# Loads of keys, values and output weights issued by GpSimd's DMA queue instead of SyncE's, in a one-core decode kernel

## The chip, the core and the metric

The kernel runs on one core of one Trainium2 chip. The metric is the device time of one execution in microseconds (us); the kernel before takes 1325.38 us, the median of three runs that lie between 1325.36 and 1325.40 us.

## The reference

One token for each of two batch elements passes through an attention block with a long cache and through a small MLP block; a gate mixes the two. Cut to what matters:

```python
# x (2,1,1024); k_cache, v_cache (2,32,16384,128); wq (1024,4096); wo (4096,1024)
# w1, w2 (1024,1024); w3 (1024,3584); w4 (3584,1024), all bfloat16
g = sigmoid((x * gate_w).sum(-1, keepdims=True))
q = (x @ wq) as (2 batch, 32 heads, 1, 128)
scores = einsum("bhqd,bhkd->bhqk", q, k_cache) * 128 ** -0.5
o = einsum("bhqk,bhkd->bhqd", softmax(scores), v_cache)
a = (o as (2, 1, 4096)) @ wo
h = gelu(layernorm(x) @ w1)              # its four column blocks are shifted along a
hs = concat(shifted blocks of h) @ w2    # sequence of length 1, so that zeros remain
x1 = x + hs
b = x1 + gelu(layernorm(x1) @ w3) @ w4
out = g * a + (1 - g) * b
```

Keys and values are 268.4 MB each (2 x 32 x 16384 x 128 x 2 bytes); all weights that are loaded together are some 34 MB.

## The kernel before

**Tiling.** The 64 pairs of batch element and head are worked on two heads of one batch element at a time, so there are 32 rounds, `n` = 0 to 31. A round needs one tile of keys and one of values. Each is a single load of 128 rows (partitions) of 64 KB, 8192 KB in all; a head takes 64 partitions, with 256 positions in each.

**The ring.** All large loads land in `ring`, five slots of 32 KB in each partition. A tile of keys or values takes two slots: values always slots 0 and 1, keys slots 3 and 4 in even rounds and 2 and 3 in odd ones (`k_slots`). The two halves of a key tile are used in an order (`k_order`) that frees slot 3 first. The weights take one slot each (`w_slots`): wq in 0 and 1, w2 in 2, w3 in 3 and 4, w4 in 0 and 1 again, and at the end wo in 4 and 3. w1 isn't loaded, since the shift leaves zeros.

**Loads.** `queue_load` puts every load into one list in the order of its use: wq (two loads), w2, w3 (two), w4 (two), then K(0), V(0), K(1), V(1) and so on, and wo (first half one load, second half six pieces). `pump` (L305) takes loads from the head of that list as long as their slots are free, and gives each the events it has to wait for: the last matmul that read the slot. `release`, called where the program writes such a matmul down, frees the slot and calls `pump` again. So a load's instruction stands in its engine's program at the place where its slots are released in the order of writing, and waits there for TensorE. Each slot has a semaphore (`s_ring`), each piece of wo one of `s_tail`.

**Prologue.** TensorE computes q from wq (L622), the zero rows from w2 (L510), the w3 product from both halves of w3 (L478), and the w4 product into rows (L510, 56 matmuls for each half). VectorE then adds and scales these rows (`st_bg`, L526 and L529). The last matmul on the first half of w3 and the one on the second free the slots of K(0); the last one on w4 frees those of V(0).

**A round.** GpSimd writes the query columns into `Z` (L652, two instructions; from the second round on they wait until the scores of the round before are done). VectorE transposes the key tile in place in eight pieces (L665); TensorE forms scores from each piece (L671, 64 matmuls in all; after 32 of them the first of the two slots is released, which is what K(n+1) waits for). Then comes the softmax (L681 to L698), the product with values (`do_PV`, L707, 64 matmuls, whose last one frees the slots for V(n+1)) and a small output step (`do_out`, L716 to L721). TensorE, VectorE and ScalarE run their rounds in a loop of 16 passes of two rounds; SyncE and GpSimd have them written out.

**End.** `do_aproj` multiplies the attention output with wo (L746), VectorE copies the rows (L775) and four small stores write them out.

SyncE issues every large load; ScalarE issues six small ones at the start (x and the gate weights) and two of the four stores; GpSimd issues none. After its constants GpSimd has one instruction in the prologue (L442) and the 64 of `Z`.

## Time and profile before

| what | before |
|---|---|
| median of three runs | 1325.38 us |
| span of the profiled execution, first to last instruction | 1323.6 us |
| time around the span, median less span | 1.8 us |
| moved by DMA | 570.6 MB, 431 GB/s over the span |
| packets of SyncE's DMA queue, share of 16 DMA engines | 99.7% |
| TensorE matmul busy | 784.8 us, 59% |
| VectorE busy | 660.1 us, 50% |
| ScalarE busy | 45.7 us, 3% |
| GpSimd busy | 23.6 us, 2% |
| granted TensorE clock, mean | 0.79 |

The profile covers one execution of the program. Its time is taken as the span and what lies around it: a change of the span is carried over to the median by adding the same 1.8 us. A row of the chain of waits or of the timeline begins with its start and its length in us. "SPq" is SyncE's instruction queue and "ACTq" ScalarE's; their rows are the issue of a load and not its transfer. Busy time of an engine counts neither issues of loads nor waits.

### The profile page before, as it was taken

To read this page: it belongs to the slowest core of one execution; us is meant where nothing else is said; L and a number is where in the kernel's file an instruction comes from. 1 tells how busy PE (TensorE), PEld (TensorE's weight loads), DVE (VectorE), ACT (ScalarE), POOL (GpSimd) and SP (SyncE) were. 2 spreads that over 40 slices of the span, in tenths; PEclk is the share of its full clock that TensorE was granted. 3 is DMA by queue.
4 is the path that set the end of the run, shared out by engine and by line. 5 is a ranking of instruction groups with operands and counts; after the bars stand their busy time and mean duration, and the time that the engine had idled before them with its cause. 6 is when DMAs were issued, how large, how long until landed. Compare 5 with 4: busy or idle time off the path is not lost.

```text
span 1323.6 us, 12296 instructions
## 1 busy us (share of the span) xinstructions
PE 784.8 (59%) x5235; PEld 335.4 (25%) x5235; DVE 660.1 (50%) x527; ACT 45.7 (3%) x99; POOL 23.6 (2%) x110
## 2 busy tenths in 40 slices
PE   3645557655556765555676554566656457656546
PEld 2512223222222322222232222222222222222223
DVE  1154446655444665544466554446655445665443
ACT  0000000000000000000000000000000000000000
POOL 3000000000000000000000000000000000000000
PEclk9966787777678777767877877888786788878679
DMA  9999999999999999999999999999999999999998
GB/s 404 444 422 436 436 430 434 436 434 432 434 438 432 430 442 430 430 440 430 430 440 430 430 440 430 432 438 430 434 436 430 436 436 428 440 432 438 432 430 365
DMA packets 11409, 570.60 MB, mean 431 GB/s; under 512 B 1267, under 2 KB 1795, under 8 KB 1926
## 3 DMA queue, kind: packets, MB, share of 16 engines
q1 hardware_dynamic: 11368, 570.43, 99.7%
q8 instruction: 8, 0.13, 0.0%
q14 instruction: 3, 0.02, 0.0%
q10 hardware_dynamic: 30, 0.01, 0.0%
HBM read 570.44 MB, written 0.00 MB: 431 GB/s over the span
## 4 chain that ended last, share of the span: by engine, by line
DMA 69%; PE 24%; DVE 6%; issue 1%; SPq 0%; POOL 0%
DMA ring<-in_A_k_cache_dram 65%; PE ps L671 23%; DVE ring L665 6%; DMA ring<-in_A_wo_dram 2%; DMA ring<-in_A_wq_dram 2%; PE ps L478 1%; PE ps L622 0%; DVE hsd L548 0%; PE ps L510 0%; PE ps L401 0%; SPq L329 0%; SPq L335 0%; POOL mv L442 0%; DVE orow L775 0%; DVE q_f L634 0%
## 5 line engine op out<-in xcount | busy, mean ns | idle before, releaser
L671 PE MATMUL ps<-ring,Z 128*128 128x512 bf16 x2048 | 533.6, 419 | 389.8 <-DVE ring L665 389.3
L665 DVE STREAM_TRANSPOSE ring<-ring 128x2048 f32<-128x2048 f32 x256 | 565.2, 2275 | 277.8 <-DMA ring<-in_A_k_cache_dram 277.8
L671 PEld LDWEIGHTS ps<-ring,Z 128*128 128x128 bf16 x2048 | 203.4, 104 | 707.5 <-issue 471.6
L707 PE MATMUL ps<-ring,PT_sb 128*32 128x512 bf16 x2048 | 168.2, 501 | 3.9 <-DVE recip L698 3.5
L721 DVE SCALAR_TENSOR_TENSOR OT_sb<-ps,gT,recip 128x2 f32 x32 | 7.0, 219 | 203.2 <-PE ps L718 203.2
L707 PEld LDWEIGHTS ps<-ring,PT_sb 128*32 128x32 bf16 x2048 | 67.6, 122 | 90.5 <-issue 69.1
L692 ACT ACTIVATE P_sb<-ps,negm 128x512 bf16<-128x512 f32 x32 | 22.0, 687 | 1013.9 <-DVE negm L690 1013.9
L681 DVE TENSOR_REDUCE rA<-ps 128x1 f32<-128x512 f32 x32 | 22.1, 692 | 64.1 <-PE ps L671 64.1
L696 PE MATMUL ps<-rowsum,hsel 128*128 128x1 f32 x128 | 24.4, 294 | 38.0 <-ACT P_sb L692 38.0
L694 DVE STREAM_TRANSPOSE PT_sb<-P_sb 128x512 bf16<-128x512 bf16 x32 | 22.8, 712 | 27.0 <-ACT P_sb L692 27.0
L652 POOL TENSOR_TENSOR Z<-q_f,mask 128x8 bf16<-128x8 f32 x64 | 12.3, 228 | 1212.9 <-PE ps L671 1212.9
L696 PEld LDWEIGHTS ps<-rowsum,hsel 128*128 128x128 f32 x128 | 21.7, 240 | 40.7 <-ACT P_sb L692 40.7
L683 PE MATMUL ps<-ident,rmax_bf 128*1 128x128 bf16 x32 | 6.9, 217 | 33.1 <-DVE rmax_bf L682 33.1
L716 ACT ACTIVATE acc_sb<-ps 128x512 bf16<-128x512 f32 x32 | 19.1, 597 | 199.0 <-PE ps L707 199.0
L718 PE MATMUL ps<-dsel,acc_sb 128*128 128x2 bf16 x128 | 8.1, 167 | 22.5 <-ACT acc_sb L716 22.5
L478 PE MATMUL ps<-xn_bf,ring 128*128 128x2 bf16 x224 | 14.5, 202 | 1.4 <-DVE xn_bf L444 1.4
L718 PEld LDWEIGHTS ps<-dsel,acc_sb 128*128 128x128 bf16 x128 | 5.3, 96 | 38.3 <-ACT acc_sb L716 38.3
L683 PEld LDWEIGHTS ps<-ident,rmax_bf 128*1 128x1 bf16 x32 | 2.5, 79 | 48.9 <-DVE rmax_bf L682 48.9
L478 PEld LDWEIGHTS ps<-xn_bf,ring 128*128 128x128 bf16 x224 | 14.4, 172 | 1.5 <-issue 1.4
L622 PE MATMUL ps<-xT_bf,ring 128*128 128x2 bf16 x256 | 7.1, 165 | 12.2 <-DVE xT_f L605 7.9
L684 DVE TENSOR_REDUCE m_sb<-ps 1x2 bf16<-1x128 bf16 x32 | 8.9, 279 | 9.9 <-PE ps L683 9.9
L690 DVE TENSOR_SCALAR negm<-ps,cAB 128x1 f32<-128x1 f32 x32 | 8.9, 278 | 9.2 <-PE ps L687 9.2
(98 smaller groups left out, 88.9 us busy)
## 6 DMA issues: line engine op xcount, KB each, us to landing
ring<-in_B_w_dram SPq DMA_DIRECT2D x4, 3584.0 KB, 35.3
ring<-in_A_wq_dram SPq DMA_DIRECT2D x2, 4096.0 KB, 17.5
ring<-in_A_wo_dram SPq DMA_DIRECT2D x1, 4096.0 KB, 40.2
ring<-in_B_w_dram SPq DMA_DIRECT2D x1, 2048.0 KB, 27.3
ring<-in_A_wo_dram SPq DMA_DIRECT2D x1, 2048.0 KB, 22.3
ring<-in_A_wo_dram SPq DMA_DIRECT2D x1, 1024.0 KB, 24.4
ring<-in_A_k_cache_dram SPq DMA_DIRECT2D x32, 26.9
ring<-in_A_v_cache_dram SPq DMA_DIRECT2D x32, 29.2
```

The source lines that it names most:

```text
L478: fn = lambda e, nb=nb, kl=kl: e.matmul(out_ps[:, nb, :], lhsT=cols(wv, kl, nb, nout), rhs=rhs_of(k0 + kl), start=False, stop=True, skip_g ...
L652: ev = pl.add("pool", lambda e, hp=hp: e.tensor_tensor(Z[:, :, ZO:ZO + P].rearrange("p t (i c) -> p t i c", c=32)[:, :, 2 * hp:2 * hp + 2, ...
L665: return pl.add("dve", lambda e: e.transpose(ap, ap), waits=(arrived(("k", n)),), sig=True)
L671: ev = pl.add("pe", lambda e, bp=bp: e.matmul(S_ps[:, 0:NCOL], lhsT=Z[:, bp, ZO - 2 * u:ZO - 2 * u + P], rhs=kv[:, :, bp // 2, :, bp % 2], ...
L681: e1 = pl.add("dve", lambda e: e.tensor_reduce(rA[:, :], S_ps[:, 0:NCOL], axis=AX.X, op=ALU.max), waits=(ev_S[n],), sig=True)
L683: e3 = pl.add("pe", lambda e: e.transpose(mt_ps, rmax_bf[:, :], ident[:, :]), waits=(e2,), sig=True)
L692: e7 = pl.add("act", lambda e: e.activation(P_sb[:, :], S_ps[:, 0:NCOL], ACT.Exp, bias=negm[:, 0:1], scale=scale, accum_out=rowsum[:, 0:1] ...
L694: e8 = pl.add("dve", lambda e: e.transpose(PT_sb[:, :], P_sb[:, :]), waits=(e7,), sig=True)
L696: e9 = pl.add("pe", lambda e, hp=hp: e.matmul(l_ps[:, hp:hp + 1], lhsT=hsel[:, hp, :], rhs=rowsum[:, 0:1], start=True, stop=True, skip_gro ...
L707: ev = pl.add("pe", lambda e, jj=jj, cg=cg: e.matmul(acc_ps[32 * cg:32 * cg + 32, 0:512], lhsT=PT_sb[:, 32 * jj:32 * jj + 32], rhs=vv[:, 4 ...
L716: e1 = pl.add("act", lambda e: e.activation(acc_sb[:, :], acc_ps[:, 0:512], ACT.Copy), waits=(ev_pv,), sig=True)
L718: e2 = pl.add("pe", lambda e, w=w: e.matmul(oT_ps, lhsT=acc_sb[:, w * P:(w + 1) * P], rhs=dsel[:, w, :], start=(w == 0), stop=(w == 3)), w ...
```

## The change

The loads of keys, values and wo move from SyncE's program to GpSimd's, with semaphores of their own for the slots (`s_pool`). wq, w2, w3 and w4 stay with SyncE, as do the two stores. Order of the list, slots, waits and sizes are the same.

```diff
         s_ring = [sem(f"dr{i}") for i in range(NRS)]
+        s_pool = [sem(f"dp{i}") for i in range(NRS)]
...
                 for k, fn in enumerate(fns):
-                    dsem = s_ring[slots[0]] if len(fns) == 1 else s_tail[k]
-                    dma_done[key] = dma_done[key, k] = pl.dma("sp", (lambda e, fn=fn, idx=slots[0]: fn(e, idx)), dsem,
+                    eng = "pool" if key[0] in ("k", "v", "wo") else "sp"
+                    dsem = (s_pool if eng == "pool" else s_ring)[slots[0]] if len(fns) == 1 else s_tail[k]
+                    dma_done[key] = dma_done[key, k] = pl.dma(eng, (lambda e, fn=fn, idx=slots[0]: fn(e, idx)), dsem,
                                                               waits=waits if k == 0 else ())
```

The line numbers of the changed kernel are higher by two from there on (L361 of before is L363). GpSimd's program from the end of the prologue into the first rounds, before; L442 is the last step of the layer norm, L652 writes `Z`, `e_pe` counts TensorE's steps:

```order
L280 MEMSET xrow 128x256 [waits e_pool]
L442 TENSOR_TENSOR mv<-mv,neg_half 128x2 [waits e_pool,e_dve]
L652 TENSOR_TENSOR Z<-q_f,mask 128x4x2 x2
L652 TENSOR_TENSOR Z<-q_f,mask 128x4x2 [waits e_pe]
L652 TENSOR_TENSOR Z<-q_f,mask 128x4x2
```

The same place in the changed kernel; L363 is a tile of keys and L367 one of values:

```order
L444 TENSOR_TENSOR mv<-mv,neg_half 128x2 [waits e_pool,e_dve]
L363 DMA ring<-in_A_k_cache_dram 128x32768 [waits e_pe]
L367 DMA ring<-in_A_v_cache_dram 128x32768 [waits e_pe]
L654 TENSOR_TENSOR Z<-q_f,mask 128x4x2 x2
L363 DMA ring<-in_A_k_cache_dram 128x32768 [waits e_pe]
L367 DMA ring<-in_A_v_cache_dram 128x32768 [waits e_pe]
L654 TENSOR_TENSOR Z<-q_f,mask 128x4x2 x2
```

K(0) and V(0) now stand ahead of the first `Z`, and K(n+1) and V(n+1) between `Z` of round n and `Z` of round n+1. `Z` of round n+1 has lost its own wait, since V(n+1) ahead of it waits for a later step of TensorE.

SyncE's whole program in the changed kernel; L331 are the weights, L780 the stores:

```order
L796 UNCONDITIONAL_BRANCH [waits barrier_Pool_Activation_PE_DVE_SP_release]
L331 DMA ring<-in_A_wq_dram 128x16384 x2
L331 DMA ring<-in_B_w_dram 128x8192
L331 DMA ring<-in_B_w_dram 128x14336 x2
L331 DMA ring<-in_B_w_dram 128x14336 [waits e_pe] x2
L780 DMA out_dram<-orow 2x256 [waits e_dve] x2
L168 UNCONDITIONAL_BRANCH [waits dout0,dout1]
```

Before, the loads of keys, values and wo stood between the two loads of w4 (the fifth row) and the stores. So w4 and K(0) were on one queue and are now on two. GpSimd's program at its end, in the changed kernel:

```order
L363 DMA ring<-in_A_k_cache_dram 128x32768 [waits e_pe]
L367 DMA ring<-in_A_v_cache_dram 128x32768 [waits e_pe]
L331 DMA ring<-in_A_wo_dram 128x16384
L654 TENSOR_TENSOR Z<-q_f,mask 128x4x2 x2
L331 DMA ring<-in_A_wo_dram 128x8192 [waits e_pe]
L331 DMA ring<-in_A_wo_dram 128x4096
L331 DMA ring<-in_A_wo_dram 128x2048
L337 DMA ring<-in_A_wo_dram 128x2x512
L337 DMA ring<-in_A_wo_dram 128x512 x2
```

The six pieces of the second half of wo stand behind the last `Z`; nothing is behind them.

## The prediction

> **What bounds the kernel now.** I read the page first, for the share of the DMA engines:

> ```profile
> span 1323.6 us, 12296 instructions
> DMA  9999999999999999999999999999999999999998
> q1 hardware_dynamic: 11368, 570.43, 99.7%
> HBM read 570.44 MB, written 0.00 MB: 431 GB/s over the span
> DMA 69%; PE 24%; DVE 6%; issue 1%; SPq 0%; POOL 0%
> ```

> The DMA engines are full in every slice, and nearly all of it is SyncE's queue (q1). The chain of waits gives PE 24%, but that is not work which could be saved, as its pieces in order of time show:

> ```profile
> 53.30 29.12 DMA ring<-in_A_k_cache_dram
> 82.42 0.02 issue
> 82.45 2.32 DVE ring L665
> 84.77 0.13 issue
> 84.90 9.99 PE ps L671 x32
> 94.91 26.22 DMA ring<-in_A_k_cache_dram
> ...
> 559.22 26.32 DMA ring<-in_A_k_cache_dram
> 597.36 26.88 DMA ring<-in_A_k_cache_dram
> 635.49 27.45 DMA ring<-in_A_k_cache_dram
> ...
> 1255.70 26.47 DMA ring<-in_A_k_cache_dram
> ```

> A load of keys lands at start plus length: K(0) at 82.42, the last at 1282.17. That is 1199.75 us for 31 rounds, 38.70 us a round. A round moves two tiles of 8.389 MB, so the stream runs at 433.5 GB/s and one tile takes 19.35 us. A load is under way for 26.2 us or more, so it was issued 7 us or more before its bytes could start: the transfer ahead of it was still running. **Full queue** is what bounds the kernel; the 1323.6 us of the span are 570.4 MB at 433.5 GB/s (1316 us) and some 8 us at both ends.

> What the change can do is therefore: make the stream run dry somewhere (each us of that is a us of time), change its rate, or nothing. How far ahead a load is issued comes from the timeline of two rounds and from the line views of the two loads (keys first, then values):

> ```profile
> 585.56 17.66 DVE L665 STREAM_TRANSPOSE ring<-ring 128x2048 f32<-128x2048 f32 x8 [7.61 <-DMA ring<-in_A_k_cache_dram]
> 597.36 0.33 SPq L361 DMA_DIRECT2D ring<-in_A_k_cache_dram  x1
> 605.28 0.39 POOL L652 TENSOR_TENSOR Z<-q_f,mask 128x8 bf16<-128x8 f32 x2 [38.31 <-PE ps L671]
> 614.38 0.33 SPq L365 DMA_DIRECT2D ring<-in_A_v_cache_dram  x1
> 624.27 17.66 DVE L665 STREAM_TRANSPOSE ring<-ring 128x2048 f32<-128x2048 f32 x8 [8.51 <-DMA ring<-in_A_k_cache_dram]
> 626.71 10.61 PE L671 MATMUL ps<-ring,Z 128*128 128x512 bf16 x40 [11.42 <-DVE ring L665]
> DMA to landing us min/median/max: 26.2/26.9/29.1
> DMA to landing us min/median/max: 27.9/29.2/35.4
> ```

> Less the 19.35 us of its own transfer, a load of keys has a lead of 6.9 to 9.8 us, one of values 8.5 us or more.

> **Part by part: the rounds.** Let L be the time from the end of GpSimd's wait to the first byte of its load. No row of the trace shows a load by GpSimd. From below the nearest row is SyncE's issue, 0.33 us. From above it is the longest way that a small load of another queue has taken, in the timeline of the start:

> ```profile
> 0.74 0.56 ACTq L577 DMA_DIRECT2D xg_row<-in_A_x_dram  x1
> 0.74 0.88 SPq L329 DMA_DIRECT2D ring<-in_A_wq_dram  x2
> 1.33 0.23 ACTq L578 DMA_DIRECT2D xg_row<-in_gate_w_dram  x1
> 7.87 0.62 PE L600 MATMUL ps<-ident,xg_row 3*128 3x3 bf16 x8 [7.87 <-DMA xg_row<-in_gate_w_dram]
> 24.24 3.57 PE L622 MATMUL ps<-xT_bf,ring 128*128 128x2 bf16 x128 [4.32 <-DMA ring<-in_A_wq_dram]
> ```

> The 2 KB of the gate weights took 6.5 us from issue at 1.33 to TensorE's start at 7.87, landing and company of another queue included, which L has not. I take L = 2 us, nearer to the lower end for that reason. [...]

> With L between 0.33 and 6.5 us the rounds lose nothing: the smallest lead is 6.9 us. The 64 issues cost SyncE's time, which nobody waits for, and now GpSimd's, which has 38.31 us of idle time ahead of each `Z`. The new place of `Z` costs nothing either. It stands behind V(n+1), which waits for the product with values: SyncE's issue at 614.38 marks that moment, so `Z` comes at 614.4 + 2 + 0.4 = 616.8 us, and its user, the matmul at 626.71, starts 9.9 us later. If that cover went, each us over it would cost a us a round, 31 in all.

> **The prologue.** Here two loads that were behind one another on one queue are now on two. The first row is from the list of issues (w4 is among these four loads), the others are from the timeline:

> ```profile
> ring<-in_B_w_dram SPq DMA_DIRECT2D x4, 3584.0 KB, 35.3
> 53.30 0.33 SPq L361 DMA_DIRECT2D ring<-in_A_k_cache_dram  x1
> 55.38 3.15 PE L510 MATMUL ps<-ring,GT_bf 128*2 128x256 bf16 x56 [2.11 <-DVE GT_bf L462]
> 63.15 3.15 PE L510 MATMUL ps<-ring,GT_bf 128*2 128x256 bf16 x56 [4.61 <-DMA ring<-in_B_w_dram]
> 66.35 0.33 SPq L365 DMA_DIRECT2D ring<-in_A_v_cache_dram  x1
> 66.36 1.77 DVE L526 TENSOR_TENSOR bgrow<-ps,xrow 2x256 f32<-2x256 f32 x4 [11.12 <-PE ps L510]
> 68.17 1.00 DVE L529 TENSOR_SCALAR ps<-bgrow,grow 64x256 f32<-64x256 f32 x2
> ```

> The second half of w4 landed at 63.15. Its 3.67 MB take 8.47 us at 433.5 GB/s, so it ran from 54.7; K(0), issued at 53.30, had to wait for it and ran from 63.1 to 82.42. Both together keep the engines busy until 82.5 in any order. But V(0) can only be issued when TensorE has used w4, and in the rounds nothing else is ready: K(1) waits for scores of K(0). If K(0), on a queue of its own, no longer stands behind w4, then w4 lands later, V(0) is issued later, and the stream may run dry at 82.5.

> That queues share the engines the start shows: the gate weights were through at 7.87 us, although SyncE's two loads of 4.19 MB, issued before, needed until 24.24. How two large loads share isn't shown; I bound it. From below, w4 goes first, lands at 63.15 as now, and the loss is 0. From above, K(0) goes first altogether and w4 lands at 82.5. The page of the profile counts 11368 packets on q1, which is one packet for each contiguous row of a load and 16 more for each load (10112 rows in 78 loads, and 8 for the stores). So w4 is 8 packets of 1.06 us on each of 16 engines, and K(0) 8 of 2.42 us. I take turns packet by packet. K(0) comes at 53.30 + 2 = 55.3, in the first packet of w4; from there the packets alternate, and the eighth of w4 ends at 54.7 + 8 x 1.06 + 7 x 2.42 = 80.1 us. TensorE's 56 matmuls take 3.15 us, V(0) is free to be issued at 83.3, its first byte comes at 85.3, and the engines have been empty since 82.5: **2.8 us** lost. By the upper bound it is 82.5 + 3.2 + 2 - 82.5 = 5.2 us. With L = 3 us two packets of w4 are through before K(0) comes, and it is 1.4; from L = 4 on it is nothing.

> [...]

> The shift has a second user, which adds nothing: VectorE's 2.8 us of L526 and L529 come at 83.3 instead of 66.36 and hold up the first transpose from 82.45 to 86.1, so scores are 3.6 us later and K(1) is issued at 98.5. V(0) then runs until 104.7, so K(1) is still 6 us early.

> **The end.** The second row is from the chain of waits in order of time, the others are from the timeline:

> ```profile
> 1282.19 17.66 DVE L665 STREAM_TRANSPOSE ring<-ring 128x2048 f32<-128x2048 f32 x8 [10.19 <-DMA ring<-in_A_k_cache_dram]
> 1293.84 0.33 SPq L329
> 1295.15 1.68 SPq L335 DMA_DIRECT2D ring<-in_A_wo_dram  x3
> 1320.62 0.91 PE L746 MATMUL ps<-ring,OT_sb 128*2 128x256 bf16 x8 [0.28 <-DMA ring<-in_A_wo_dram]
> 1321.05 0.95 DVE L775 CAST orow<-ps 34x256 bf16<-34x256 f32 x2 [7.42 <-PE ps L746]
> ```

> Behind the last keys (1282.2) the stream still has V(31), until 1301.5, and the first 4.19 MB of wo, until 1311.2. The pieces of the second half, issued by SyncE until 1296.8, may come 14 us later before the engines wait. Six of them at 2 us each on GpSimd after the wait at 1293.8 are issued by 1305.8: cost 0. Without that cover it would be 12 us.

> **The sum.** 1323.6 + 2.8 = 1326.4 us of span, with 1.8 us around it 1328.2 us, against a median of 1325.38. I call 0.2% (2.65 us) no change, about what a measurement of this kernel can tell; the forecast lies just beyond it.

> **Rivals.** *The stream doesn't run dry:* w4 lands early enough, because queues share by bytes (each gets half the rate, w4 then lands at about 71 and V(0) is issued at 74.5) or because GpSimd's first load takes 4 us. Then nothing changes: 1325.4 us. For it speaks that a queue's first load is the slow one at ScalarE (0.56 us to issue, the second 0.23), and that the early landing of the gate weights shows sharing but not how; against it, that a packet is the only unit of which the trace tells.

> *VectorE holds GpSimd up.* K(n+1) is issued in the middle of the eight transposes (597.36 within 585.56 to 603.22). If GpSimd could not write its load's program until they are done, the round would be 17.66 us of transposes, L, and 19.35 us of transfer: 37.0 + L. That decides from L = 1.7 us on. At L = 2 it is 0.3 us a round, 9 us in all (1335); at L = 3 it is 1.3 us a round, 40 us (1366). No row shows GpSimd at work during a transpose, so the trace says neither yes nor no. [...] A transpose of 2048 elements takes 2.2 us here (17.66 for eight), just under one element a ns.

> *The software queue is slower itself.* If one of 16 engines lags by 0.5 to 2%, each tile does, and 64 tiles of 19.35 us make 6 to 25 us: 1332 to 1350. No row speaks for it. [...]

> *Faster:* the change from one load to the next costs SyncE's queue something, and GpSimd's less. At 0.3% of the 1238 us of tiles that is 3.7 us: 1321.7. No row shows a gap between tiles, so little is to be had.

> **Chances.** The forecast (a gap of 1.4 to 5.2 us, L up to 3 us; 1326.8 to 1330.6) has 0.50; no dry stream 0.22; VectorE's hold 0.10; a slower queue 0.08; a faster one 0.10. Of the forecast's 0.50 I put 0.29 above 1328.03 us, the bound of 0.2%. So slower is 0.29 + 0.10 + 0.08 = 0.47, same 0.21 + 0.22 = 0.43, faster 0.10. The range reaches from 1324, which leaves out the faster case (0.10), to 1340, which takes in the small ends of the two slow cases and leaves out some 0.10.

> **What would show it.** In the changed kernel's timeline the second group of L512 (L510 of before) starts at about 80 and not at 63, V(0) is issued at 83, and a slice near 83 to 85 us has idle DMA engines; from there everything is later by the same amount, with rounds of 38.70 us. L is read off at the first load that finds the engines empty. A round of more than 38.8 us proves the prediction wrong and one of the two slow rivals right: VectorE's hold if keys start only after the last transpose, the queue if tiles take over 19.4 us while two are in flight. L512 at 63 us with the old time means that nothing ran dry.

## The result and the profile after

The changed kernel takes 1328.03 us (median of 18 runs, 1327.42 to 1328.79), the kernel before 1325.40 us (18 runs beside them, 1325.24 to 1325.55). The ratio is 1.002, with a 95% interval from 1.0014 to 1.0026: slower by 2.6 us, just at the bound of 0.2%. The profiled execution has a span of 1326.6 us, 3.0 more than before. The forecast was 1328.2 us and 1326.4 us of span. So the total is as forecast; its parts are not, as the rest shows, and that the total agrees is in part luck.

The page of the changed kernel, its lines on DMA and the shares of the chain:

```profile
span 1326.6 us, 12296 instructions
DMA  9999999999999999999999999999999999999998
q0 software_dynamic: 9968, 545.26, 95.1%
q1 hardware_dynamic: 1016, 25.17, 4.5%
DMA 68%; PE 24%; DVE 6%; issue 1%; POOL 0%; SPq 0%
```

The stream now is GpSimd's queue (q0), and it is as full as SyncE's was (430 GB/s over the span, 431 before). A loss of 3 us does not show in slices of 33 us. It shows in the chain of waits, in order of time, where a load of keys lands at start plus length:

```profile
53.45 29.00 DMA ring<-in_A_k_cache_dram
94.14 28.39 DMA ring<-in_A_k_cache_dram
134.66 26.58 DMA ring<-in_A_k_cache_dram
...
1179.44 26.89 DMA ring<-in_A_k_cache_dram
1217.58 28.11 DMA ring<-in_A_k_cache_dram
1257.73 26.68 DMA ring<-in_A_k_cache_dram
```

| landing | before | after | later by |
|---|---|---|---|
| K(0) | 82.42 | 82.45 | 0.03 |
| K(1) | 121.13 | 122.53 | 1.40 |
| K(2) | 159.82 | 161.24 | 1.42 |
| K(29) | 1204.76 | 1206.33 | 1.57 |
| K(30) | 1243.47 | 1245.69 | 2.22 |
| K(31) | 1282.17 | 1284.41 | 2.24 |
| end of span | 1323.6 | 1326.6 | 3.0 |

The loss thus comes in three steps: 1.40 us between K(0) and K(1), 0.65 in one late round, and 0.8 behind the last load. The 28 rounds from K(1) to K(29) add 0.17 us together. The first step is in the timeline of the changed kernel:

```profile
53.45 0.73 POOL L363 DMA_DIRECT2D ring<-in_A_k_cache_dram  x1 [15.20 <-PE ps L480]
75.23 3.15 PE L512 MATMUL ps<-ring,GT_bf 128*2 128x256 bf16 x56 [16.98 <-DMA ring<-in_B_w_dram]
78.72 0.54 POOL L367 DMA_DIRECT2D ring<-in_A_v_cache_dram  x1 [24.54 <-PE ps L512]
82.47 17.66 DVE L667 STREAM_TRANSPOSE ring<-ring 128x2048 f32<-128x2048 f32 x8 [1.22 <-DMA ring<-in_A_k_cache_dram]
```

The second half of w4 is there at 75.23 us (63.15 before), V(0) is issued at 78.72 (66.35 before), and the transposes start as soon as K(0) lands. The rows of the view of DMA that count the packets started from 78 to 98 us, first before, then after:

```profile
DMA packets 145, 8.45 MB, mean 423 GB/s; under 512 B 16, under 2 KB 16, under 8 KB 16
```

```profile
DMA packets 133, 7.62 MB, mean 381 GB/s; under 512 B 16, under 2 KB 16, under 8 KB 16
```

Thirteen packets of 64 KB are missing in this stretch, and there is one fetch of instructions more, of 16 KB at 80.1 us (five of the thirteen come in the next 20 us, where the starts fall otherwise): here the stream loses its time. In the records of single packets the engines end K(0) one by one between 79.9 and 82.1 us, and V(0)'s first packets start between 80.2 and 82.2, so that between the two loads an engine goes 0.35 us on average without a packet of either. But nearly all of the first two packets of V(0) on each engine take 2.5 to 3.9 us instead of 2.42, and that is another 1.15 us an engine. Most of the loss is slow first packets, and only the smaller part is engines that stand empty. K(0) is used 0.4 us after the last engine is through with it (82.07 and 82.47 us), so a landing can be later by more or less than the 16 engines are on average; here K(1) is 1.40 us later by its landing and 1.37 by the average.

The last step is at L168, where each engine has a DRAIN and behind it an EVENT_SEMAPHORE. Before, then after:

```profile
L168 POOLq DRAIN  x1: 486/486/486, 1263.2 to 1263.2; - x1
L168 SPq DRAIN  x1: 7/7/7, 1323.4 to 1323.4; - x1
```

```profile
L168 POOLq DRAIN  x1: 28295/28295/28295, 1298.1 to 1298.1; - x1
L168 SPq DRAIN  x1: 7/7/7, 1325.7 to 1325.7; - x1
```

GpSimd's DRAIN took half a microsecond in the middle of the last rounds; now it takes 28.3 us and ends at 1326.4, after SyncE's, so that all wait for it: the EVENT_SEMAPHOREs of the other four, at 1323.6 before, are at 1326.5 and 1326.6. Its end lies 3.41 us behind the last packet of the software queue (1322.97). K(31) is 2.24 us late and SyncE's DRAIN 2.3, so nearly all of the 0.8 us behind the last load is this wait.

### The profile page after: what moved, and what is told of

Its sections match the earlier page's. It is cut to its first block, busy times and chain, and to the rows that moved or that the text cites. A ratio compares the mean times of both kernels' runs of the same rounds, so it can differ in the third digit from the quotient of the medians.

```text
span 1326.6 us, 12296 instructions
## 1 busy us (share of the span) xinstructions
PE 784.0 (59%) x5235; PEld 333.9 (25%) x5235; DVE 659.9 (50%) x527; ACT 45.7 (3%) x99; POOL 62.9 (5%) x181
## 2 busy tenths in 40 slices
DMA  9999999999999999999999999999999999999998
## 3 DMA queue, kind: packets, MB, share of 16 engines
HBM read 570.44 MB, written 0.00 MB: 430 GB/s over the span
## 4 chain that ended last, share of the span: by engine, by line
DMA 68%; PE 24%; DVE 6%; issue 1%; POOL 0%; SPq 0%
DMA ring<-in_A_k_cache_dram 65%; PE ps L673 22%; DVE ring L667 6%; DMA ring<-in_A_wo_dram 2%; DMA ring<-in_A_wq_dram 2%; PE ps L480 1%; PE ps L624 0%; DVE hsd L550 0%; PE ps L512 0%; PE ps L403 0%; POOL ring L331 0%; PE ps L748 0%; POOL mv L444 0%; DVE orow L777 0%; DVE q_f L636 0%
## 5 line engine op out<-in xcount | busy, mean ns | idle before, releaser
L363 POOL DMA_DIRECT2D ring<-in_A_k_cache_dram x32 | 18.3, 573 | 649.2 <-PE ps L673 634.0
L367 POOL DMA_DIRECT2D ring<-in_A_v_cache_dram x32 | 16.9, 528 | 540.1 <-PE ps L709 515.6
L512 PE MATMUL ps<-ring,GT_bf 128*2 128x256 bf16 x112 | 6.1, 406 | 19.2 <-DMA ring<-in_B_w_dram 17.0
L624 PE MATMUL ps<-xT_bf,ring 128*128 128x2 bf16 x256 | 7.1, 165 | 12.1 <-DVE xT_f L607 7.9
## 6 DMA issues: line engine op xcount, KB each, us to landing
ring<-in_B_w_dram SPq DMA_DIRECT2D x4, 3584.0 KB, 38.9
```

Of the source, the lines that this page charges most:

```text
L363: queue_load(("k", n), [lambda e, idx: e.dma_start(ring[:, idx:idx + 2, :].rearrange("p s m -> p (s m)"), kv_src(A_k, n))], k_slots[n % 2])
L367: queue_load(("v", n), [lambda e, idx: e.dma_start(ring[:, idx:idx + 2, :].rearrange("p s m -> p (s m)"), kv_src(A_v, n))], (0, 1))
```

## The experiments

Three questions were open: whether two queues or the software queue cost the 1.4 us; how long before the engines run out a load has to be issued; and what ties the DRAIN down.

### One queue or two

**K(0) on ScalarE's queue**, no load on GpSimd:

```diff
-                    dma_done[key] = dma_done[key, k] = pl.dma("sp", (lambda e, fn=fn, idx=slots[0]: fn(e, idx)), dsem,
+                    dma_done[key] = dma_done[key, k] = pl.dma("act" if key == ("k", 0) else "sp", (lambda e, fn=fn, idx=slots[0]: fn(e, idx)), dsem,
```

> The kernel before, with K(0) alone issued on ScalarE's hardware queue; GpSimd issues nothing. Theory now (what costs is that K(0) and w4 are on two queues, whichever they are: w4 lands late, V(0) is issued within 2 us of the first engine's running empty, and its first packets are slow): w4 lands at 75 to 80 us, V(0) is issued at 78 to 83, K(1) lands 1.4 us late or more, 1326.8 to 1328.5, as with K(0) alone on GpSimd (1327.0). Rival (it is the software queue): 1325.4.

```profile
77.51 3.01 PE L510 MATMUL ps<-ring,GT_bf 128*2 128x256 bf16 x56 [19.01 <-DMA ring<-in_B_w_dram]
80.57 0.33 SPq L365 DMA_DIRECT2D ring<-in_A_v_cache_dram  x1
122.94 8.89 DVE L665 STREAM_TRANSPOSE ring<-ring 128x2048 f32<-128x2048 f32 x4 [9.30 <-DMA ring<-in_A_k_cache_dram]
```

Measured: 1327.68 us (11 runs, 1327.19 to 1328.11), ratio 1.0017 (1.0008 to 1.0026). In its timeline w4 is late, and K(1) is used at 122.94, 1.8 us later than before. So this much is lost with SyncE's and ScalarE's queues too, without a load on GpSimd's.

**K(0) alone on GpSimd**, all else on SyncE (GpSimd passes its arrival on to the semaphore that the others wait for):

```diff
+                    eng = "pool" if key == ("k", 0) else "sp"
...
+                pl.add("pool", lambda e: e.sem_inc(s_ring[k_slots[0][0]], 16), waits=tuple(fwd))
```

> Only K(0) is issued by GpSimd; V(0), all later tiles and wo stay with SyncE. Theory (the stream loses time because V(0) is issued late, with w4 held up by K(0), and then needs GpSimd's long way to its first byte): w4 still lands at about 75 us, but SyncE issues V(0) at 78.5 and needs 1.0 us to the first byte (as its first load of the kernel: issue 0.74, first packet 1.77), so V(0) is there before the first engine is empty at 79.9. K(1) lands at 121.1 to 121.4 as before, and the time is 1325.4 to 1325.8. Rival 1 (two queues that share cost time by themselves, whoever issues V(0)): K(1) at 122.5, 1326.8. Rival 2 (GpSimd's queue costs in the rounds and at the end): 1325.4.

```profile
75.06 3.16 PE L517 MATMUL ps<-ring,GT_bf 128*2 128x256 bf16 x56 [16.52 <-DMA ring<-in_B_w_dram]
78.26 0.33 SPq L372 DMA_DIRECT2D ring<-in_A_v_cache_dram  x1
84.84 17.66 DVE L672 STREAM_TRANSPOSE ring<-ring 128x2048 f32<-128x2048 f32 x8 [3.76 <-POOLq L767]
97.18 0.33 SPq L368 DMA_DIRECT2D ring<-in_A_k_cache_dram  x1
```

Measured: 1327.03 us (1325.66 to 1327.70), ratio 1.001 (1.0001 to 1.0019). The theory, that nothing is lost when SyncE issues V(0), fell: SyncE issues it at 78.26, 0.04 us behind the last matmul on w4 (GpSimd takes 0.34), and in the profiled run (1327.10 us) K(1) is as late as in the changed kernel (1.45 us). The first rival stood, but not for all of the loss: averaged over the 16 engines K(1) is only 0.73 us late (1.37 in the changed kernel), and five of the eleven runs took 1326.15 us or less, the other six 1327.03 or more. So with SyncE as the issuer about half of the average loss is left; the other half went with the issuer or with the 0.5 us by which V(0) is issued earlier, which no run tells apart. The end costs nothing here: K(31) is 1.65 us late and the span 1.7 us longer, and GpSimd's DRAIN takes 0.58 us. The transposes start late because the last of K(0)'s 4-byte packets (more on these below) came at 84.47, behind a packet of V(0); K(1) is issued at 97.18 for that reason, and its packets lose nothing by it.

**w4 on GpSimd too**, one queue for w4 and K(0), but w3 on the other:

```diff
-                    eng = "pool" if key[0] in ("k", "v", "wo") else "sp"
+                    eng = "pool" if key[0] in ("k", "v", "wo", "w4") else "sp"
```

> As the changed kernel, but w4 too is loaded by GpSimd, so that w4 and K(0) are on one queue again, one behind the other, and w4 shares the engines with wq, w2 and w3 on SyncE's queue. Theory (two queues alternate packet by packet, and a load that frees the next one is slowed): w3, which frees K(0)'s slots, now lands at about 62 us instead of 46, K(0) is issued at about 70, the stream has run dry since 63, and K(0) lands at 92 to 94 instead of 82.4; everything is later by about 11 us, and the time is 1335 to 1338 us. Rival 1 (the loss of the changed kernel is that w4 and K(0) were on different queues, and nothing else): then it is gone, 1325.4 to 1326.2 us. Rival 2 (a queue that was first keeps its turn, so that w3 is hardly slowed): 1326 to 1329 us.

The timeline, and the row of a table by stretches whose last columns are the granted clock, the share of the DMA engines and GB/s:

```profile
63.20 7.26 PE L480 MATMUL ps<-xn_bf,ring 128*128 128x2 bf16 x112 [3.46 <-DMA ring<-in_B_w_dram]
70.76 0.57 POOL L363 DMA_DIRECT2D ring<-in_A_k_cache_dram  x1 [27.17 <-PE ps L480]
94.27 17.66 DVE L667 STREAM_TRANSPOSE ring<-ring 128x2048 f32<-128x2048 f32 x8 [13.19 <-DMA ring<-in_A_k_cache_dram]
```

```profile
66.00:72.00 6.00, 4.46 (x71) 4.37 (x69) 1.05 (x6) 0.25 (x1) 0.57 (x1) 1.00 0.00 0
```

Measured: 1338.31 us (4 runs, 1338.12 to 1338.56), ratio 1.0098 (1.0082 to 1.0113), 0.3 us above the range. The landings are 11.8 us late from K(0) to K(31). Now w3 is the load that is slowed, the load behind it comes 17 us later, and the engines stand still. This is the mechanism of the prologue with a loss eight times as large: a load that frees the slots of the next one is slowed by one that could have stood behind it.

**All but wq on GpSimd**, so that w4 and K(0) are on one queue and w3 as well:

```diff
-                    eng = "pool" if key[0] in ("k", "v", "wo") else "sp"
+                    eng = "sp" if key[0] == "wq" else "pool"
```

> As the changed kernel, but w2, w3 and w4 are loaded by GpSimd too, ahead of K(0) in the same queue; only wq stays with SyncE. Theory (two queues with large loads cost, and the software queue by itself only the end): w2 is issued at about 15.2 us, when GpSimd has written its constants, still during wq; from about 25 us one queue feeds the engines, in the order of before. w4 lands at 63 to 64 us, V(0) is issued at 66 to 67 and K(0) and K(1) land within 0.3 us of before (82.4 and 121.1). Only the 0.8 us of the last DRAIN are left: 1325.9 to 1326.5 us, with runs that lie within 0.4 us. Rival 1 (the software queue as such costs the start, with whatever it stands beside): K(1) is 1.4 us later than before and the time 1327.6 to 1328.6 us, as in the changed kernel.

```profile
63.25 3.16 PE L512 MATMUL ps<-ring,GT_bf 128*2 128x256 bf16 x56 [4.60 <-DMA ring<-in_B_w_dram]
66.73 0.54 POOL L367 DMA_DIRECT2D ring<-in_A_v_cache_dram  x1 [12.47 <-PE ps L512]
121.28 8.89 DVE L667 STREAM_TRANSPOSE ring<-ring 128x2048 f32<-128x2048 f32 x4 [8.50 <-DMA ring<-in_A_k_cache_dram]
```

Measured: 1326.67 us (11 runs, 1326.36 to 1328.38), ratio 1.0011 (1.0002 to 1.002), span 1324.7. The landings are as the theory has them: w4 at 63.25, all keys 0.13 to 0.15 us later than before. The software queue by itself costs 0.14 us at the start, nothing in the rounds, and about 1.0 us at the end. The median is 0.2 us above the expected range and the runs spread over 2 us; the profiled run shows no reason for the spread.

### When the load comes

**K(0) waits until the gelu result is written** (55.3 us), 2.4 us later than in the changed kernel:

```diff
-                       k_slots[n % 2])
+                       k_slots[n % 2] + (("gate",) if n == 0 else ()))
...
-        put([gelu2])
+        def open_gate():
+            slot_free["gate"] = (evd["GT"],)
+            pump()
+        put([gelu2, open_gate])
```

> The changed kernel with K(0) held until the gelu result (55.3 us). Theory: K(0) is issued at 55.5 and its first packet comes 4 us later, when one or two packets of w4 are left on each engine: w4 lands at 66 to 68 us, V(0) is issued at 70 to 71, 9 us before an engine is empty, so neither K(0) nor V(0) comes to an engine that has run out. K(1) lands at 121.1 to 121.5, and only what is lost outside the prologue stays: 1326.0 to 1326.8. Rival (a first load by GpSimd costs its 1.4 us in any place): 1328.0.

```profile
55.86 0.73 POOL L363 DMA_DIRECT2D ring<-in_A_k_cache_dram  x1 [17.62 <-DVE GT_bf L464]
70.28 3.16 PE L512 MATMUL ps<-ring,GT_bf 128*2 128x256 bf16 x56 [11.75 <-DMA ring<-in_B_w_dram]
73.77 0.54 POOL L367 DMA_DIRECT2D ring<-in_A_v_cache_dram  x1 [17.18 <-PE ps L512]
121.06 11.08 DVE L670 STREAM_TRANSPOSE ring<-ring 128x2048 f32<-128x2048 f32 x5 [8.49 <-DMA ring<-in_A_k_cache_dram]
```

Measured: 1326.09 us (11 runs, 1326.03 to 1326.27), ratio 1.0005 (0.9996 to 1.0014), as expected. More packets of w4 go ahead of K(0) than in the changed kernel; w4 lands at 70.28 us, later than the expected 66 to 68, and V(0) is issued at 73.77, still early enough: all landings up to K(31) are those of before within 0.1 us. What is left is the end. This is the fastest kernel with GpSimd's loads, 1.9 us below the changed one and 0.7 above before.

**K(0) waits until the first half of w4 is used** (58.6 us); the gate is the same, opened there:

```diff
+            if key == ("w4", 0):
+                slot_free["gate"] = (ev,)
```

> All of the changed kernel, but K(0) waits in addition until the first half of w4 has been used (58.5 us), so that with 4 us to its first byte it comes as the second half of w4 ends. Theory: no sharing, w4 lands at 63 to 64 us, V(0) is issued at 67, K(1) lands at 121.1 to 121.6, the 1.4 us of the prologue are gone, and 1.2 us of the 2.6 stay: 1326.6. If all that was lost came from the prologue: 1325.4. Rival (it is spread over rounds and end, the prologue being chance): 1328.0.

```profile
58.92 0.73 POOL L365 DMA_DIRECT2D ring<-in_A_k_cache_dram  x1 [20.68 <-PE ps L514]
62.96 3.16 PE L514 MATMUL ps<-ring,GT_bf 128*2 128x256 bf16 x56 [4.36 <-DMA ring<-in_B_w_dram]
84.29 17.66 DVE L669 STREAM_TRANSPOSE ring<-ring 128x2048 f32<-128x2048 f32 x8 [15.31 <-DMA ring<-in_A_k_cache_dram]
```

Measured: 1328.25 us (1327.12 to 1328.93), ratio 1.0021 (1.0012 to 1.003), against 1326.6 expected. w4 and V(0) are in time now, but K(0), issued 4.0 us before w4 was through, lands 1.85 us late: coming so shortly before the other queue is empty loses as much here as the changed kernel does (1.40).

**K(0) waits for w4 to land, on GpSimd's queue and on SyncE's.** The same edit on the changed kernel and on the one before:

```diff
+                if key == ("k", 0):
+                    waits += (dma_done["w4", 1],)
```

> The changed kernel with K(0) held until the second half of w4 has landed (63.15 us): the stream is dry for as long as GpSimd's load needs to start. Theory (time from dry to the first byte is 4.05 us as at K(0), and two first packets are slow by 0.6 us each): K(0) lands 5.3 us later than the 82.4 of before, and this passes whole to the end: 1325.4 + 5.3 + 1.2 = 1331.9. With 1.6 us, the shortest that V(0) shows: 1329.5. Rival (a delay of the stream is made up later): 1326 to 1327.

> The kernel before with K(0) held in the same way, issued by SyncE. Theory (1.0 us to the first byte, one first packet slow by 0.65 us): K(0) lands 1.8 us later, 1327.2. The difference to the kernel with GpSimd is the price of a start by GpSimd on an empty stream, 3.5 us without the 1.2 us that are not of the prologue. Rival (made up later): 1325.4.

GpSimd's first, then SyncE's:

```profile
63.54 0.73 POOL L365 DMA_DIRECT2D ring<-in_A_k_cache_dram  x1 [25.29 <-DMA ring<-in_B_w_dram]
86.18 17.66 DVE L669 STREAM_TRANSPOSE ring<-ring 128x2048 f32<-128x2048 f32 x8 [17.19 <-DMA ring<-in_A_k_cache_dram]
```

```profile
63.13 0.33 SPq L363 DMA_DIRECT2D ring<-in_A_k_cache_dram  x1
85.75 17.66 DVE L667 STREAM_TRANSPOSE ring<-ring 128x2048 f32<-128x2048 f32 x8 [16.64 <-DMA ring<-in_A_k_cache_dram]
```

Measured: 1331.12 us (ratio 1.0044, 1.003 to 1.0057) and 1329.44 us (1.0031, 1.0019 to 1.0043). From issue to use it is 22.6 us in both, 3.3 us more than the transfer of a full stream. The way to the first packet is only 1.4 us of it on GpSimd's queue and 1.0 on SyncE's. The engines then start over 1.0 and 1.2 us, the first packet on each takes about 3.1 us in place of 2.42, and the use comes 0.4 to 0.5 us behind the last packet. So a dry start makes K(0) 3.3 us late on SyncE's queue, where 1.8 were expected, and 3.7 on GpSimd's, where the expected 4 us to the first packet did not come about. By K(31) the landing is 3.8 and 4.8 us late; the average of the 16 engines does not grow (3.7 and 4.6 us at K(0), 3.6 and 4.5 at K(30)), only the last engine falls back further.

**Keys always late.** In both kernels the two slots of a key tile are released together at the end of the scores, so that every load of keys finds the engines empty:

```diff
-                release(("k", n), ev, (slots_of["k", n][u // UH],))
+                halves.append(u // UH)
+                if last:
+                    for hf in halves:
+                        release(("k", n), ev, (slots_of["k", n][hf],))
+                    del halves[:]
```

> The changed kernel, with both slots of K(n) released only at the end of its scores, so that K(n+1) is issued 8 us later in every round and the stream is empty when it comes. Theory: a load by GpSimd lands 22.6 us after its issue when it finds the engines empty (as with K(0) held until w4 had landed), and the issue comes 20.05 us after the landing of the last keys: 42.7 us a round in place of 38.7, 31 rounds, 1449 us. Rival (the software queue needs 4 us to its first byte in the rounds too): 45.1 us a round, 1525 us.

> The kernel before with the same late release. Theory: 22.6 us from issue to landing, as SyncE's K(0) when held, and the issue 19.75 us after the last landing: 42.35 us a round, 1438 us. The difference to GpSimd's run is then 0.3 us a round: what GpSimd adds on an empty stream is its wait, not its descriptors. If GpSimd's way were the longer one by 2.5 us: some 80 us of difference.

The lists of issues, the last column the median from issue to landing; GpSimd's, then SyncE's:

```profile
ring<-in_A_k_cache_dram POOLq DMA_DIRECT2D x32, 22.2
```

```profile
ring<-in_A_k_cache_dram SPq DMA_DIRECT2D x32, 21.9
```

Measured, one run each: 1437.03 and 1415.81 us, rounds of 42.2 and 41.6 us (31 rounds, from K(0)'s landing to K(31)'s). Both are shorter than expected; the difference is 0.7 us a round. About 0.3 us of it is in this view and the rest is GpSimd's later issue (19.95 us behind the landing, SyncE's 19.68) and what follows from both. That is all that the software queue costs in a round of this kernel where no cover is left.

### The end

Both are made from the kernel in which K(0) waits for gelu. **All of wo on SyncE:**

```diff
-                    eng = "pool" if key[0] in ("k", "v", "wo") else "sp"
+                    eng = "pool" if key[0] in ("k", "v") else "sp"
```

> As the kernel in which K(0) waits for the gelu result (1326.09 us), but wo is loaded by SyncE, all of it. Theory (two queues alternate packet by packet): SyncE is free to issue the first half of wo at 1271, in the middle of K(31), where before it stood behind V(31). K(31) then lands at about 1287 instead of 1282.2, V(31) at 1311 to 1314 instead of 1301.5, the product with values starts then and not at 1305.7, and the end is about 4 us later: 1328 to 1330.5 us, although GpSimd's last DRAIN no longer costs its 0.8 us. Rival 1 (only the DRAIN matters at the end): 1325.2 to 1325.6 us. Rival 2 (the DRAIN is not tied to the software queue's last packet and stays): 1326.1 us.

From the chain of waits, and the view of L168:

```profile
1255.34 35.22 DMA ring<-in_A_k_cache_dram
```

```profile
L168 POOLq DRAIN  x1: 42488/42488/42488, 1272.5 to 1272.5; - x1
L168 SPq DRAIN  x1: 7/7/7, 1329.6 to 1329.6; - x1
```

Measured: 1331.62 us (5 runs, 1329.73 to 1333.21), ratio 1.0043 (1.003 to 1.0057), 1 us above the range. SyncE issued the first half of wo already at 1263.05 and not at 1271, since the slot is free after K(30)'s scores; K(31) lands at 1290.6, 8.4 us late, and scores, softmax and everything behind are late. GpSimd's DRAIN ends at 1315.0, 3.7 us behind V(31)'s last packet of data, and nobody waits for it. Two loads that share, not the DRAIN, decide this kernel.

**Only the second half of wo on SyncE:**

```diff
-                    eng = "pool" if key[0] in ("k", "v", "wo") else "sp"
+                    eng = "pool" if (key[0] in ("k", "v") or key == ("wo", 0)) else "sp"
```

> As the kernel in which K(0) waits for the gelu result (1326.09 us), but the second half of wo (six pieces) is loaded by SyncE; the first half stays with GpSimd behind V(31). Theory: the software queue's last packet is then at about 1317 instead of 1320.8, GpSimd's DRAIN ends 3.4 us behind it, at about 1320.4, ahead of the last step of the others; sharing delays V(31) by about 2 us and the first half of wo by about 4 us, both hidden. What the software queue cost is then all gone: 1325.2 to 1325.6 us, the time of the kernel before. Rival 1 (the DRAIN goes with GpSimd's having issued loads at all): 1326.1 us. Rival 2 (the sharing at the end is not hidden): 1326.5 to 1328 us.

```profile
1316.65 5.26 PE L751 MATMUL ps<-ring,OT_sb 128*2 128x256 bf16 x128 [3.46 <-DMA ring<-in_A_wo_dram]
```

```profile
L168 POOLq DRAIN  x1: 45381/45381/45381, 1273.9 to 1273.9; - x1
L168 SPq DRAIN  x1: 7/7/7, 1324.2 to 1324.2; - x1
```

Measured: 1326.72 us (11 runs, 1325.98 to 1327.65), ratio 1.0011 (1.0002 to 1.002). The DRAIN went as the theory has it: it ends at 1319.3, 3.4 us behind the queue's last packet, out of the way. The time did not: the first half of wo is slowed by the second, TensorE waits for it until 1316.65, its 128 matmuls then need 5.26 us, and the span is 1324.4 us as without the edit. The second rival's mechanism took the place of the DRAIN.

## Why the prediction was right, and where it was not

**The full queue and the rounds: right.** The rounds lose nothing: 0.17 us in 28 of them. The loads of keys still take 26.0 us or more from issue to landing, so the smallest lead is 6.6 us. The line view of L363:

```profile
L363 POOL DMA_DIRECT2D ring<-in_A_k_cache_dram x32: 567/567/726, 53.4 to 1257.7; - x32
DMA to landing us min/median/max: 26.0/26.8/29.0
```

This also settles two rivals, which were suppositions that no row of before showed. GpSimd is not held up by the transposes: K(n+1) is issued in the middle of them, in 0.57 us (the longest issue of keys took 0.73). And the software queue is neither slower nor faster: the round is 38.70 us, and a packet of 64 KB takes 2.42 us on both queues.

**The prologue: the sharing was right, the size was off by a factor of two, by errors against each other.** w4 was predicted at 80.1 us and landed at 75.2. The packets do alternate, as the prediction took them to: in the records, from 57.3 us on, each of the 16 engines has one packet of K(0) behind each one of w4, until w4's last row at 72.4. One row is one packet (8192 packets of 64 KB for the 64 tiles of 128 rows), and the upper bound, K(0) first altogether and w4 at 82.5, did not come about.

K(0)'s first packets came 3.9 to 5.3 us after its issue and not 2, while on empty engines they came after 1.4 to 2.5 (K(0) held until w4 has landed); in between each engine began three or four more packets of w4. Why a load takes longer to its first packet in company isn't shown. It is not a fixed number of packets: where wo came beside K(31), with packets of 64 KB in place of 28, it took 3.4 to 4.9 us as well (the kernel with all of wo on SyncE).

By the prediction's own formula L = 4 gives 75.3, but that agreement is luck too. The second half of w4 began between 52.0 and 53.9 us and not at 54.7, and its last row was through at 72.4. Behind the data of each large load the records have one packet of 4 bytes on each engine (9 ns; 16 of them behind w4 and 16 behind K(0)); these are the 16 more packets of the prediction, which gave them no turn. They came up to one packet of K(0) later, the last at 74.8, and TensorE's wait for w4 ended 0.4 us after it, as it does in the kernel before (62.7 and 63.15). So up to 2.4 us of w4's 12.1 us went by when its bytes were already there.

By the same formula V(0), issued 3.7 us before K(0) landed, should have cost nothing. It cost 1.4. The step that failed is that the stream loses only the time in which the engines are empty, all of them at one moment, so that a load needs a lead of L and no more. The engines ran out one by one from 79.9 to 82.1 us and went 0.35 us on average without a packet, so the idle slice that was to show it is hardly there; V(0)'s slow first packets took the other 1.15 us, and the sum had no term for them. Why they are slow isn't shown. In the runs the loss goes with the lead, here counted from the issue to 0.4 us behind the last bytes of what is queued ahead (where it lands when nothing holds up its 4-byte packets). The third figure is the delay of the landing that follows (K(0)'s or K(1)'s), the fourth how much later the 16 engines are through with the load itself on average:

| load | queue | lead, us | landing later by, us | engines later by, us |
|---|---|---|---|---|
| keys of the rounds, changed kernel | GpSimd | 6.6 or more | 0.0 | 0.0 |
| V(0), K(0) held until gelu | GpSimd | 8.6 | 0.0 | 0.1 |
| V(0), K(0) alone on GpSimd | SyncE | 4.0 | 1.45 | 0.75 |
| K(0), held until half of w4 is used | GpSimd | 4.0 | 1.85 | 1.3 |
| V(0), changed kernel | GpSimd | 3.7 | 1.40 | 1.4 |
| V(0), K(0) on ScalarE | SyncE | 1.7 | 1.8 | 1.8 |
| K(0), held until w4 has landed | SyncE | -0.1 | 3.3 | 3.7 |
| K(0), held until w4 has landed | GpSimd | -0.6 | 3.7 | 4.6 |

In these runs a lead of 4 us is too short and 6.6 is enough. With less the cost rises to 3.3 us and more at no lead, of which the way to the first packet is about a third.

So V(0) was issued 4.6 us earlier than predicted, which by the prediction's sum takes away all of its 2.8 us, and the slow start, which the sum put at nothing, cost 1.4. That the span still grew by 3.0 us, close to the 2.8 of the forecast, is luck: 0.65 us in a late round and 0.8 at the end, for which the forecast had nothing, made up for what the prologue lacked.

**The first rival** (no dry stream, because GpSimd's first load takes 4 us) had its condition fulfilled, since K(0)'s first packet did come after some 4 us, and still did not come about: V(0)'s lead was too short.

**VectorE's 2.8 us ahead of the first transpose** did not hold it up: w4 was early enough for them to be done by 81.25 us.

**The end: predicted 0, measured 0.8 us.** The pieces of wo were hidden as predicted; what was not thought of is GpSimd's DRAIN, which with the last loads on GpSimd's queue ends 3.4 us behind the last packet (SyncE's DRAIN took 7 ns when the last loads were on SyncE's). SyncE's DRAIN, behind the last matmuls, the copy and the stores, is there 2.7 us behind that packet, at 1325.7. Where GpSimd's last load is done earlier (K(0) alone on GpSimd, either edit of the end) its DRAIN is not the last.

**The late round:** the 0.65 us between K(29) and K(30) belong to one engine. The packet records have an 8 KB fetch of instructions of 0.31 us at 1242.2 us, and the packet of 64 KB behind it takes 2.77 us instead of 2.42: 0.66 us together, on the engine that was last at that moment. The average of the 16 engines hardly moves (1.29 us late before, 1.33 after). Three other kernels with GpSimd's loads have the same fetch, with the same 2.77 us behind it, between 1239.9 and 1244.0 us (K(0) held until gelu, until half of w4 is used, and until w4 has landed); there it hits an engine that was not last, and the round is longer by 0.1 us or nothing. Before, the fetch fell at 1300.5, behind the last keys. So this step is not the sharing of the prologue, and it need not be in every run; the times of the changed kernel are 1.4 us apart (before 0.3). Medians give 2.6 us, of which 1.4 + 0.8 are the prologue and the end. Whether the place of such fetches is why some of the kernels with two queues spread by 1 to 3.5 us, and the one held until gelu by 0.24, stays open.

## What to carry to other kernels

In this kernel two large loads on two queues share the DMA engines packet by packet, so a load that others wait for, or that frees the slots of the next one, is slowed by a bulk load that could have stood behind it (w4 landed at 75.2 us and not at 63.15): keep both on one queue in the order of need (0.14 us instead of 1.4), or hold the bulk load back a little (0.1 us), but not until the other load ends (1.85 us). A full stream lost nothing here with its next load 6.6 us ahead or more; 4.0 us was too late on either queue (1.45 us on SyncE's, 1.85 on GpSimd's), and a stream that had run dry cost 3.3 us on SyncE's and not just the 1.0 us to the first packet. When you look for lost time, look at the lengths of the packets too and not only for idle engines, and ask whether all engines are late or only the last one. GpSimd's queue itself is as fast as SyncE's in these rounds (2.42 us for a packet of 64 KB on both); give its last load time before the end, since here its DRAIN ended 3.4 us behind.
